# A sliding-window attention with a routed expert layer: keys in a ring, loads and stores on queues of their own, a token table built by matrix products, logits in float32

## The chip, the cores and the metric

The kernel runs on one core of a Trainium2 chip (trn2). The metric is the device time of one execution in microseconds (us), lower is better. The kernel before took 771.98 us in the median of 3 runs (769.98 to 776.52). One more execution was recorded by the profiler; it took 768.93 us.

## What is computed

The reference, cut to what matters:

```python
# q, k, v: (8 batches, 8 heads, 576, 64), float32
scores = q @ k.T / 8
mask_plain = (rel >= 0) & (rel < 32)                       # heads 0 to 3
mask_dil = (rel >= 0) & (rel < 128) & (rel % 4 == 0)       # heads 4 to 7
attn = softmax(where(mask, scores, -1e9)) ; out = attn @ v
x = out.transpose(0, 2, 1, 3).reshape(4608, 512)
logits = x @ w_gate                                        # 8 experts
e = argmax(logits) ; gate = softmax(logits)[e]
y = gate * (relu(x @ w1[e]) @ w2[e])                       # 512 -> 1024 -> 512
```

Each of the 4608 tokens goes to one expert only. Which one depends on the data, so the kernel has to make lists of tokens by expert on the chip.

## The kernel before, in words

There are two stages: 36 tiles of attention with the routing beside them, and then the expert layer.

**Attention.** A tile holds 128 query positions of all 8 heads (two batches side by side, `NPR` = 4 pairs of batches, `NT` = 9 tiles each). `step(n)` (L790) is a pipeline over tiles: in step n PE computes the scores of tile n (`st_scores`, L220, 32 query rows against a window of 64 keys, 16 matmuls), the product with the values of tile n-2 (`st_av`, L267), the transposes of the probabilities of n-1 (`st_trans`), those of the outputs of n-3 (`st_xt`, L317), the logits of n-4 (`st_logits`, L336) and the mask of n+1. DVE computes `nm` (the row maximum), `d` (scores less maximum), `z`, `rz`, `xs` (the normalised output) and `xtl`; ACT computes exp and copies out of PSUM (`pts`, `xth`, `lgs`). The order on PE, DVE and ACT is the program's own up to step 34 (`manual_schedule`, L825); later a scheduler sets it.

SP issues the transfers, in program order: `load(n)` (L164) brings the queries `qt` (256 KB) and, in two transfers, `kvb`: 64 partitions of 640 key columns and 1040 value columns each, where the keys of a tile come with the 32 keys before them. `st_x` (L292) writes the output `xs` to `x_d` in DRAM, in two or three transfers, since the dilated heads (L307 to L315) run through the sequence by residue classes. In `step`, `load(n + 2)` stands behind `st_x(n - 2)`, so on SP the load stands behind the writes. Eight weight tiles of expert 0 (`raw`, 512 KB each) are loaded in between and split into a high and a low part (`wu`).

**Routing.** Logits are computed from a high and a low part of x in a reduced-precision float32 (`xth`, `xtl`, 8 matmuls per tile). After each pair of batches `route` (L388) finds for each token its expert, its gate and its slot (the running place in the list of its expert), in some 15 small DVE operations, spread over the steps (`on_pe`, `off_pe`, `pull_pe`, `pull_off`, L357 to L374). `place` (L425) then scatters a pair (row, gate) of 8 bytes for each token into the DRAM `table`: one indirect DMA on POOL for each tile of 128 tokens, 36 in all. The scatters of three pairs serve the early part of expert 0 (`first`, 3 blocks of 128 tokens), whose `fetch_x` (L568) reads `it` back from `table`, gathers the rows `xg` of `x_d` by it (POOL), and has PE transpose them (`tpx`, L582).

**Experts.** For each expert `layer1` (L608, tile `hps`) and `layer2` (L640, tile `yps`) run over blocks of 128 tokens, with weights and activations split in high and low parts (3 matmuls for one). DVE makes the low parts (`wu` L517, `h` L630). Tokens beyond 512 of an expert go to `Dynamic` blocks (L659), whose table rows and weights are gathered by POOL. `finish` (L550) multiplies by the gate and scatters 128 rows of the output.

Of the kernel before, what the change touches and what calls it, by code (L numbers as in the profile page):

```python
# [9 lines left out]
F32 = mybir.dt.float32  # L10
# [26 lines left out]
KW = P + W  # L37
KC = HP * KW
VC = NB * HP * (DH + 1)
BIG = float(2.0**100)  # L40

SLOTS = 512
CAP = N + SLOTS
# [6 lines left out]
C_ID, C_TRI, C_ONE, C_REV, C_C0, C_BASE, C_THR, C_PU, C_NEW, C_D, C_P = np.cumsum(  # L50
    [0, P, P, P, NE, NE, NE, NTHR, NE, NE * NT, DBLK]
).tolist()
C_ALL = C_P + 1


def _constants():
# [12 lines left out]
    tok = np.zeros((P, NPR, NT, 2), np.int32)  # L69
    tok[:, :, :, 0] = (  # L70
# [5 lines left out]
    slot = np.zeros(((NE + 1) * CAP, 2), np.int32)  # L76
    slot[:, 0] = np.arange((NE + 1) * CAP) % DUMMY

    pos = np.arange(S2) % S
    key = (pos // W * W - W)[:, None] + np.arange(2 * W)[None, :]  # L80
    rel = pos[:, None] - key
    plain = (rel >= 0) & (rel < W) & (key >= 0)
    dil = plain & (key // CLS == (pos // CLS)[:, None])
    mask = np.where(np.stack([plain, dil], axis=1), 0.0, -BIG)
    mask = mask.reshape(NT, P, 2 * 2 * W).transpose(1, 0, 2).reshape(P, -1)
    mask = np.concatenate([np.eye(P), mask], axis=1)
    mask = mask.astype(mybir.dt.np(BF16))
    return dict(cst=c, tok=tok, slot=slot, mask=mask, zero=np.zeros((DUMMY, DM), np.float32))


def _layout(q, k, v, wg, w1, w2):
    perm = np.arange(S).reshape(CLS, DIL).T.reshape(-1)

    def ordered(a):

        a = np.concatenate([a[:, : H // 2], a[:, H // 2 :][:, :, perm]], axis=1)
        return a.reshape(NPR, 2, HP, 2, S, DH).transpose(0, 2, 3, 1, 4, 5).reshape(
            NPR, HP, 2, S2, DH
        )

    def padded(a):
        return np.pad(ordered(a), ((0, 0), (0, 0), (0, 0), (W, 0), (0, 0)))

    qt = ordered(q).reshape(NPR, HP, 2, NT, P, DH).transpose(0, 3, 5, 2, 1, 4)
    kp, vp = padded(k), padded(v)
    kw = np.stack([kp[:, :, :, P * t : P * t + KW] for t in range(NT)], axis=1)
    kw = kw.transpose(0, 1, 3, 5, 2, 4).reshape(NPR * NT, 2, DH, KC)
    vp = np.concatenate([vp, np.ones_like(vp[..., :1])], axis=-1)
# [9 lines left out]
        axis=1,  # L118
    )
    w = np.ascontiguousarray(w).reshape(NE * 8 * P, DF)  # L120
    return dict(
        q=qt.reshape(NPR * NT, P, HP * P), kv=np.concatenate([kw, vw], axis=-1), wg=wgt, w=w
    )

# [896 lines left out]
```

## Time and profile before

| what | value |
|---|---|
| median of 3 runs | 771.98 us |
| profiled execution, its own time | 768.93 us |
| span of that execution, first to last instruction | 767.2 us |
| PE busy | 633.6 us (83% of the span) |
| DVE, ACT, POOL busy | 378.3, 292.7, 186.3 us |
| bytes moved by DMA | 135.77 MB, 177 GB/s in the mean |
| scores of the last tile | about 251 us after the start |
| first matmul of the experts | about 289 us after the start |

Busy time of an engine says little by itself, since the two stages have different limits: the experts keep PE busy without a gap, attention does not. So the profile is read by stage: when the tiles of attention come, what PE waits for between them, what the DMA engines move then, and when the first matmul of the experts starts. "DMA share" is the time that packets took, as a share of 16 engines. "PEclk" is the granted clock as a share of 2.4 GHz; 0.5 is 1.2 GHz.

### The profile page before, as it was taken

What the parts mean: (1) busy time and instruction counts of PE and PEld (TensorE: products, weight loads), DVE (VectorE), ACT (ScalarE), POOL (GpSimd) and SP (SyncE); (2) the same over time, 40 slices, a digit from 0 to 9 for tenths busy, and PEclk for the clock granted to TensorE, in tenths of its full rate; (3) what the DMA queues carried; (4) which work ended last, traced back from release to release, by engine and by line L of the source; (5) the groups of instructions that cost most, each with busy time, mean ns of one, the idle gap of its engine ahead of it and who ended that gap; (6) DMA issues with size and microseconds to landing.
All of it is one profiled execution on the core that took longest, in us unless ns stands there. A gap on an engine that the chain in (4) does not pass through costs nothing. (4 is left out here: it accounts for less than half of the span.)

```text
span 767.2 us, 12980 instructions
## 1 busy us (share of the span) xinstructions
PE 633.6 (83%) x5096; PEld 524.6 (68%) x5096; DVE 378.3 (49%) x708; ACT 292.7 (38%) x564; POOL 186.3 (24%) x184
## 2 busy tenths in 40 slices
PE   4666671765667529999999999999999999999992
PEld 3555661665566429877888888888888888888881
DVE  3555652564355426172663663563654564564410
ACT  1333331332233222262562662653653554554410
POOL 4000031004000414343144044044144134133010
PEclk9999996886687858999999999999999999999997
DMA  8777778778775534254655555565565465565010
GB/s 310 258 248 252 230 229 71 266 257 174 135 256 192 76 102 104 84 166 164 196 202 170 201 193 179 186 211 168 188 214 174 158 228 162 176 229 172 27 42 29
DMA packets 51775, 135.77 MB, mean 177 GB/s; under 512 B 12496, under 2 KB 21840, under 8 KB 51664
## 3 DMA queue, kind: packets, MB, share of 16 engines
q1 hardware_dynamic: 36032, 85.06, 37.7%
q0 software_dynamic: 15680, 49.86, 19.9%
q8 instruction: 41, 0.67, 0.4%
q14 instruction: 22, 0.18, 0.1%
HBM read 115.19 MB, written 20.59 MB: 177 GB/s over the span
## 5 line engine op out<-in xcount | busy, mean ns | idle before, releaser
L517 DVE TENSOR_TENSOR wu<-raw,wu 128x512 fp32r<-128x512 f32 x224 | 144.1, 688 | 81.2 <-ACT wu L516 76.7
L619 PE MATMUL hps<-x,wu 128*128 128x512 f32 (+1 forms) x768 | 179.2, 392 | 2.5 <-DVE h L630 1.9
L649 PE MATMUL yps<-wu,h 128*128 128x512 f32 x744 | 179.4, 396 | 0.0
L619 PEld LDWEIGHTS hps<-x,wu 128*128 128x128 f32 x768 | 144.4, 191 | 31.7 <-DVE h L630 2.3
L649 PEld LDWEIGHTS yps<-wu,h 128*128 128x128 f32 x744 | 139.1, 188 | 31.9
L516 ACT CAST wu<-raw 128x512 fp32r<-128x512 f32 x224 | 126.3, 618 | 75.1 <-DMA raw<-in_w_dram,wi 37.3
L225 PE MATMUL s<-kvb,qt 128*32 128x128 f32 x1152 | 50.0, 327 | 90.6 <-DMA kvb<-in_kv_dram 90.6
L225 PEld LDWEIGHTS s<-kvb,qt 128*32 128x32 f32 x1152 | 38.0, 130 | 100.0 <-issue 88.3
L426 POOL DMA_INDIRECT table<-pay,pos x36 | 36.4, 1012 | 243.5 <-DVE pay L363 158.2
L630 DVE SCALAR_TENSOR_TENSOR h<-hps,h 128x512 fp32r<-128x512 f32 (+1 forms) x64 | 42.8, 672 | 79.6 <-ACT h L629 79.5
L264 ACT COPY pts<-pt 128x512 f32<-128x512 f32 x36 | 21.1, 586 | 158.6 <-PE pt L260 151.5
L692 POOL DMA_INDIRECT raw<-in_w_dram,wi x56 | 56.5, 1009 | 82.4 <-DVE wu L517 70.1
L629 ACT ACTIVATE h<-hps 128x512 fp32r<-128x512 f32 (+1 forms) x64 | 37.0, 582 | 94.1 <-PE hps L619 94.1
L236 DVE TENSOR_REDUCE nm<-s 128x8 f32<-128x512 f32 x36 | 24.8, 689 | 87.1 <-PE s L225 87.1
L554 POOL DMA_INDIRECT out_dram<-y,it x31 | 31.8, 1026 | 133.1 <-DVE y L553 116.9
L274 PE MATMUL o<-kvb,pts 128*32 128x130 f32 x1152 | 50.8, 323 | 0.9 <-DVE xs L295 0.9
L740 PE MATMUL ypd<-wu,hd 128*128 128x512 f32 x192 | 51.4, 405 | 0.0
L542 POOL DMA_INDIRECT xg<-x_d,it x31 | 29.7, 959 | 67.5 <-DMA it<-table 35.9
L709 PE MATMUL hpd<-wu,xd 128*128 128x512 f32 x192 | 46.0, 395 | 0.0
L274 PEld LDWEIGHTS o<-kvb,pts 128*32 128x32 f32 x1152 | 43.1, 132 | 2.3 <-ACT lgs L355 0.9
L553 DVE TENSOR_SCALAR y<-yps,it 128x256 f32<-128x256 f32 x31 | 15.0, 483 | 59.1 <-ACT y L552 59.1
L709 PEld LDWEIGHTS hpd<-wu,xd 128*128 128x128 f32 x192 | 36.0, 188 | 8.7 <-DVE xd L686 0.2
(99 smaller groups left out, 623.4 us busy)
## 6 DMA issues: line engine op xcount, KB each, us to landing
raw<-in_w_dram SPq DMA_DIRECT2D x64, 512.0 KB, 4.6
kvb<-in_kv_dram SPq DMA_DIRECT2D x72, 420.0 KB, 5.3
qt<-in_q_dram SPq DMA_DIRECT2D x36, 256.0 KB, 3.1
x_d<-xs SPq DMA_DIRECT2D x44, 128.0 KB, 3.2
x_d<-xs SPq DMA_DIRECT2D x8, 112.0 KB, 5.3
raw<-in_w_dram,wi POOLq DMA_INDIRECT x56, 5.2
x_d<-xs SPq DMA_DIRECT2D x8, 96.0 KB, 2.3
x_d<-xs SPq DMA_DIRECT2D x8, 80.0 KB, 1.8
```

The source lines that it names most:

```text
L225: nc.tensor.matmul(s[W * j : W * (j + 1), h], lhsT=qt[:, h, W * j : W * (j + 1)], rhs=kt[:, :, o : o + 2 * W], start=False, stop=h == HP - 1,)
L274: nc.tensor.matmul(st["o", n][W * j : W * (j + 1), h // 2, h % 2 * 2 : h % 2 * 2 + 2], lhsT=pts[:, h, W * j : W * (j + 1)], rhs=kt[:, :, a ...
L426: i = nc.gpsimd.indirect_dma_start(out=table, out_offset=bass.IndirectOffsetOnAxis(ap=pos[:, t : t + 1], axis=0), in_=pay[:, b, t, :], in_ ...
L516: nc.scalar.copy(u[:, 0, sl], raw[:, sl])
L517: nc.vector.tensor_tensor(u[:, 1, sl], raw[:, sl], u[:, 0, sl].bitcast(F32), op=ALU.subtract)
L619: nc.tensor.matmul(hps[:, : self.ns], lhsT=u[:, wpart, fs], rhs=self.x[:, xpart, c, : self.ns], start=(k == 0), stop=(k == 11),)
L629: nc.scalar.activation(h[:, 0, :n], hps[:, :n], AF.Relu)
L630: nc.vector.scalar_tensor_tensor(h[:, 1, :n], hps[:, :n], 0.0, h[:, 0, :n].bitcast(F32), op0=ALU.max, op1=ALU.subtract,)
L649: nc.tensor.matmul(yps, lhsT=self.h[f][:, hpart, ts], rhs=u[:, wpart, fs], start=(k == 0), stop=(k == 23),)
L692: nc.gpsimd.indirect_dma_start(out=raw, out_offset=None, in_=w, in_offset=bass.IndirectOffsetOnAxis(ap=self.wi[:, u : u + 1], axis=0),)
L709: nc.tensor.matmul(hps, lhsT=self.x[:, xpart, c], rhs=u[:, wpart, ns], start=(k == 0), stop=(k == 11),)
L740: nc.tensor.matmul(yps, lhsT=self.h[f // 4][:, hpart, f % 4], rhs=u[:, wpart, fs], start=(k == 0), stop=(k == 23),)
```

## The change

- **Keys in a ring.** A tile's 128 keys are loaded once into a ring of 5 places (`kring`); the scores read the 32 keys before them from the neighbour's place (`keys`, an access pattern with a step between the two halves). The dilated heads are laid out so that a tile is 128 consecutive positions for all heads.
- **Queues.** SP carries loads: `load_qk(n + 3)` behind `st_scores(n)`, `load_v(n + 1)` behind `st_av(n - 2)`, queries in 3 buffers, values in 3. `x_d` is written from the ACT queue, in two transfers per tile (`st_xout`).
- **Logits** in plain float32: 4 matmuls per tile into four 32-partition groups, one copy `xt` instead of `xth` and `xtl`, and two copies out (`st_keep`); the sum over the four groups is a product with a 0/1 matrix (`turn`, 9 matmuls for a pair of batches).
- **Table.** Slots are cut in block (slot & -128) and place (slot & 127). For each of 36 tiles DVE makes `s1` (128 x 128, one-hot by place, times the token number) and `b1` (128 x 320, one-hot by block), and PE adds `s1`ᵀ`b1` into `tb` in PSUM; `tbl` sums over the pairs, and `decode` turns it to row numbers `row_i` in SBUF. `table`, its 36 scatters and the reads `it` and `itd` are gone. Gates go to a DRAM column `g_d`, and each block gathers its 128 gates by an indirect DMA (`gates`). Dynamic blocks find their rows in `row_i` by 7 pairs of DVE operations.
- Route's tiles, `d` and `p` have one buffer instead of two.

```diff
-            nc.sync.dma_start(kvb[n % NKV][i::2, i], kv[n, i])
+            nc.sync.dma_start(kring[i::2, n % NK, i], k[n, i])
+
+    def load_v(n):
+        if not 0 <= n < total:
+            return
+        for i in range(2):
+            nc.sync.dma_start(vb[n % NV][i::2, i], v[n, i])
...
+    def st_xout(n):
+        xs, lo = st["xs", n], DUMMY + n * P
+        rows = x_d[lo : lo + P]
+        nc.scalar.dma_start(rows[:, : DM // 2], xs[:, 0].rearrange("p h d -> p (h d)"))
+        nc.scalar.dma_start(
+            rows[:, DM // 2 :].rearrange("(r j) d -> j r d", j=DIL),
+            xs[:, 1].rearrange("p h d -> p (h d)"),
+        )
...
+        def mark(t):
+            s1 = sp.tile([P, P], F32R, name="s1", bufs=3)
+            b1 = sp.tile([P, NBK], F32R, name="b1", bufs=3)
+            v.tensor_scalar(
+                s1,
+                ca[:, C_IO - C_TRI : C_IO + P - C_TRI],
+                plc[:, t : t + 1],
+                pay[:, m, t : t + 1],
+                op0=ALU.is_equal,
+                op1=ALU.mult,
+            )
+            v.tensor_scalar(
+                b1, cc[:, C_BK - C_ATT : C_BK + NBK - C_ATT], blk[:, t : t + 1], None, op0=ALU.is_equal
+            )
...
+                nc.tensor.matmul(box["tb"], lhsT=s1, rhs=b1, start=t == 0, stop=t == NT - 1)
...
+    def gates(it_col, to, rows=N):
+        nc.gpsimd.indirect_dma_start(
+            out=to,
+            out_offset=None,
+            in_=g_d[: DUMMY + rows],
+            in_offset=bass.IndirectOffsetOnAxis(ap=it_col, axis=0),
+        )
...
         go(st_scores, n)
+        load_qk(n + 3)
         go(st_av, n - 2)
+        load_v(n + 1)
...
-        load(n + 2) if n else None
...
+        go(st_xcopy, n - 3)
+        go(st_xout, n - 2)
```

The order on SP in the middle of attention; before, for two tiles (L303 and L311 are the writes of `x_d`):

```order
L303 DMA x_d<-xs 128x256
L311 DMA x_d<-xs 80x256
L311 DMA x_d<-xs 48x256
L168 DMA qt<-in_q_dram 128x512
L170 DMA kvb_105<-in_kv_dram 64x1680 x2
L303 DMA x_d<-xs 128x256
L311 DMA x_d<-xs 96x256
L311 DMA x_d<-xs 32x256
L168 DMA qt<-in_q_dram 128x512
L170 DMA kvb_106<-in_kv_dram 64x1680 x2
```

With the change (L182 queries, L184 keys, L190 values, L652 a weight tile):

```order
L652 DMA raw<-in_w_dram 128x1024
L182 DMA qt<-in_q_dram 128x512
L184 DMA kring<-in_k_dram 64x512 x2
L190 DMA vb_110<-in_v_dram 64x1040 x2
L182 DMA qt<-in_q_dram 128x512
L184 DMA kring<-in_k_dram 64x512 x2
L190 DMA vb_111<-in_v_dram 64x1040 x2
```

No write stands on SP any more, and a tile has five loads there instead of three.

The order on POOL from its first work to the first blocks of expert 0, before:

```order
L176 MEMSET kvb_106 128x3360
L176 MEMSET kvb_107 128x3360
L426 DMA table<-pay,pos 46080x2 x27
L542 DMA xg<-x_d,it 128x512 x3
L426 DMA table<-pay,pos 46080x2 x9
L671 DMA itd<-table,ti_3362 128x2
```

and with the change:

```order
L198 MEMSET vb_111 128x2080
L199 MEMSET wgz 128x128
L586 DMA xg<-x_d,row_i 128x512 x3
L595 DMA gate<-g_d,row_i 128x1 x3
L586 DMA xg<-x_d,row_i 128x512 x2
L595 DMA gated<-g_d,row_i 128x1
```

The 36 scatters are gone, and gathers of gates stand among those of the rows.

The order on DVE where the last pair of batches is routed, beside the first matmuls of the experts. Before (`pos` is the slot, `h` the low part of a result of layer 1, `wu` of a weight):

```order
L466 TENSOR_TENSOR sel<-rk,oh 128x72
L476 TENSOR_TENSOR crun<-crun,cs 128x8
L517 TENSOR_TENSOR wu<-raw,wu 128x512
L469 TENSOR_REDUCE posf<-sel 128x9
L881 TENSOR_TENSOR cnt<-tot,cc 128x8
L363 CAST pos<-posf 128x9
L630 SCALAR_TENSOR_TENSOR h<-hps,h 128x384
```

With the change, the end of the same stretch (the seven pairs of `s1` and `b1` before these stand between `pos` and them):

```order
L440 TENSOR_SCALAR s_3362<-ca,plc,pay 128x128
L448 TENSOR_SCALAR b_3363<-cc,blk 128x320
L440 TENSOR_SCALAR s_3366<-ca,plc,pay 128x128
L448 TENSOR_SCALAR b_3367<-cc,blk 128x320
L504 TENSOR_TENSOR tbl<-tbl,tb 128x320
L515 TENSOR_SCALAR scr<-tbl 128x320
L519 TENSOR_SCALAR none<-tbl,ca 128x320
L516 SCALAR_TENSOR_TENSOR scr<-tbl,scr 128x320
L949 TENSOR_TENSOR cnt<-tot,cc 128x8
L522 TENSOR_TENSOR row_i<-scr,none 128x320
L680 SCALAR_TENSOR_TENSOR h<-hps,h 128x384
```

Before, the first `h` came right behind `pos`; now nine pairs of marks, the sum into `tbl` and the four operations of `decode` stand between the two.

## Rows read from the trace of the kernel before

**Rows 1.** Page, part 2: busy tenths of PE in 40 slices of 19.2 us.

```profile
PE   4666671765667529999999999999999999999992
```

**Rows 2.** Stages: window, its us, busy us of each engine, PEclk, DMA share, GB/s.

```profile
16.00:112.00 96.00, 65.16 (x1275) 56.59 (x1277) 55.88 (x118) 31.69 (x67) 3.73 (x4) 0.91 0.78 253
112.00:137.00 25.00, 8.41 (x146) 6.78 (x141) 6.86 (x13) 4.31 (x9) 5.79 (x6) 0.70 0.83 106
...
181.00:206.00 25.00, 9.70 (x150) 8.72 (x150) 7.20 (x14) 3.36 (x8) 7.66 (x8) 0.62 0.93 160
...
251.20:289.00 37.80, 14.49 (x176) 11.31 (x174) 12.98 (x27) 10.10 (x22) 11.26 (x11) 0.65 0.44 93
...
320.00:767.20 447.20, 431.22 (x1959) 349.41 (x1957) 223.27 (x362) 204.03 (x378) 134.45 (x134) 0.98 0.51 167
```

**Rows 3.** Waits up to 420 us: engine, line, releaser: total us, times, longest.

```profile
PE s L225 <- DMA kvb<-in_kv_dram: 90.6, 27, 16.3
```

**Rows 4.** Timeline of DVE: starts of the row maxima (tiles 3, 18, 19, 26, 28, 35).

```profile
22.09 0.69 DVE L236 TENSOR_REDUCE nm<-s 128x8 f32<-128x512 f32 x1 [1.60 <-PE s L225]
...
116.73 0.69 DVE L236 TENSOR_REDUCE nm<-s 128x8 f32<-128x512 f32 x1 [0.62 <-PE s L225]
...
137.18 0.69 DVE L236 TENSOR_REDUCE nm<-s 128x8 f32<-128x512 f32 x1 [12.32 <-PE s L225]
...
179.87 0.68 DVE L236 TENSOR_REDUCE nm<-s 128x8 f32<-128x512 f32 x1
...
204.79 0.69 DVE L236 TENSOR_REDUCE nm<-s 128x8 f32<-128x512 f32 x1 [8.28 <-PE s L225]
...
252.60 0.68 DVE L236 TENSOR_REDUCE nm<-s 128x8 f32<-128x512 f32 x1
```

**Rows 5.** Waits of SP up to 300 us, same columns.

```profile
SPq L303 <- DVE xs L295: 106.2, 34, 6.8
```

**Rows 6.** Timeline of SP: start, us, what; one tile's writes.

```profile
48.83 0.33 SPq L303 DMA_DIRECT2D x_d<-xs  x1
49.21 0.95 SPq L311 DMA_DIRECT2D x_d<-xs  x2
```

**Rows 7.** DMA issues: line, engine, xcount, KB each, median us to landing.

```profile
kvb<-in_kv_dram SPq DMA_DIRECT2D x72, 420.0 KB, 5.3
...
x_d<-xs SPq DMA_DIRECT2D x44, 128.0 KB, 3.2
...
table<-pay,pos POOLq DMA_INDIRECT x36, 14.0
```

**Rows 8.** Stages of 2 us at the start, columns as in rows 2.

```profile
14.00:16.00 2.00, 2.00 (x34) 1.53 (x27) 1.04 (x4) 0.63 (x1) 0.00 (x0) 1.00 1.14 466
```

**Rows 9.** Timeline of PE: two masks, one step apart.

```profile
44.79 0.39 PE L211 MATMUL s<-mk 128*128 128x512 bf16 x1
...
48.42 0.39 PE L211 MATMUL s<-mk 128*128 128x512 bf16 x1
```

**Rows 10.** Timeline, all engines, from attention's end to the first expert matmul.

```profile
273.00 0.39 SPq L571 DMA_DIRECT2D it<-table  x1
...
275.83 0.97 POOL L542 DMA_INDIRECT xg<-x_d,it  x1 [13.84 <-DMA it<-table]
...
280.65 1.12 PE L582 MATMUL tpx<-ident,xg 128*128 128x128 f32 x4 [14.50 <-DMA xg<-x_d,it]
...
289.02 1.33 PE L619 MATMUL hps<-x,wu 128*128 128x384 f32 x3 [0.68 <-ACT x L585]
```

**Rows 11.** Groups up to 300 us: line, engine, shapes, xcount | busy us, mean ns.

```profile
L331 DVE TENSOR_TENSOR xtl<-tp,xth 128x512 fp32r<-128x512 f32 x36 | 24.9, 691 | 26.5 <-ACT xth L326 25.7 <-issue 0.6
...
L444 DVE TENSOR_TENSOR sh<-lg,mx 128x72 f32<-128x72 f32 x4 | 0.9, 224 | 0.0
...
L883 DVE TENSOR_TENSOR over<-cnt,cc 128x320 f32<-128x320 f32 x1 | 0.5, 480 | 0.0
```

**Rows 12.** Groups from 289 to 320 us, same columns.

```profile
L619 PE MATMUL hps<-x,wu 128*128 128x384 f32 x96 | 19.3, 359 | 0.7 <-ACT x L585 0.7
```

More of the change, by code (lines that the diff above doesn't have):

```diff
@@ L218, in st_mask, with keys @@
         st["s", n] = s
+    def keys(n, h, j):
+        here, last = n % NK, (n - 1) % NK
+        cols = slice(h * P + W * j, h * P + W * (j + 1))
+        if h < HP // 2 and j:
+            return kring[:, here, :, h * P + W * (j - 1) : h * P + W * (j + 1)]
+        own = kring[:, here, :, cols]
+        before = kring[:, last, :, cols] if h >= HP // 2 else kring[:, last, :, (h + 1) * P - W : (h + 1) * P]
+        (part, rows), (head, two), (one, _) = own.ap
+        step = own.offset - before.offset
+        return bass.AP(own.tensor, before.offset, [[part, rows], [head, two], [step, 2], [one, W]])
     def st_scores(n):
-        s, qt, kt = st["s", n], qts.pop(n), kvb[n % NKV]
+        s, qt = st["s", n], qts.pop(n)
         for h in range(HP):
             for j in range(NB):
-                o = h * KW + W * j
                 nc.tensor.matmul(
@@ L419, in rank @@
             )
-            nc.tensor.matmul(
-                rk, lhsT=cc[:P, C_TRI : C_TRI + P], rhs=oh, start=False, stop=False
-            )
-            nc.tensor.matmul(rk, lhsT=one, rhs=cs, start=False, stop=True)
-        def place(t):
-            i = nc.gpsimd.indirect_dma_start(
-                out=table,
-                out_offset=bass.IndirectOffsetOnAxis(ap=pos[:, t : t + 1], axis=0),
-                in_=pay[:, b, t, :],
-                in_offset=None,
-            )
-            tc.declare_no_dep(i.ins, group="slots", reason="slots are handed out once")
-            need(i, [table_init])
-            tc.add_to_no_dep_group("slots", i.ins)
-            scatters.append(i)
@@ L569, in fetch_x @@
             e = self.e
-            self.it = sp2.tile([P, 4, 2], I32, name="it")
-            i = nc.sync.dma_start(
-                self.it[:, : self.nblk],
-                table[e * CAP : e * CAP + self.ns].rearrange("(i p) t -> p i t", p=P),
-            )
-            need(i, scatters)
-            self.xg = [gather(self.it[:, i, 0:1], self.rows) for i in range(self.nblk)]
+            self.it = [row_i[:, e * BPE + i : e * BPE + i + 1] for i in range(self.nblk)]
+            self.xg = [gather(it, self.rows) for it in self.it]
+            self.gate = sp2.tile([P, 4], F32, name="gate")
+            for i, it in enumerate(self.it):
+                gates(it, self.gate[:, i : i + 1], self.rows)
             self.x = pools["x", e % 2].tile([P, 2, 4, SLOTS], F32R, tag="x", name="x")
```

411 lines of the change are left out of this document (219 added, 192 removed).

## The prediction, made blind

> **What bounds the kernel now.** I read the page first, for where PE is not busy [rows 1]: in slices 1 to 15 it is 40 to 70% busy, with two holes at slices 7 and 10 and one at slice 14, and from slice 16 on it is full. So the kernel is attention, some 250 us, a hole of nearly 40 us, and then the experts, which PE bounds: from 320 us to the end it is busy 431.22 us of 447.20, and most of what is left over is the drain of the last stores [rows 2].
>
> Next the stages. While the tiles of attention run undisturbed (16 to 112 us), PE is busy 65 us of 96 and DVE 56; neither is full. The DMA share is 0.78, at 253 GB/s [rows 2]. The waits say who is late: PE stood 90.6 us before the scores for `kvb`, in 27 waits [rows 3]. That SP had not issued the loads earlier is seen in its own queue: before the write of `x_d` it waited 106.2 us for `xs`, 34 times [rows 5], and the load of tile n+2 stands behind that write. So a load starts late in step n, needs 5.3 us to land [rows 7], and must be there at the start of step n+2.
>
> The row maxima give the pace: from tile 3 at 22.09 to tile 18 at 116.73 us are 15 steps of 6.31 us [rows 4]. A step in which PE waits for nothing is 48.42 - 44.79 = 3.63 us [rows 9].
>
> The holes at slices 7 and 10 are the scatters. Tile 18 to 19 took 20.45 us and tiles 26 to 28 24.92 us [rows 4], against 6.31 and 12.62: together 26.4 us lost. In these stretches the DMA share is 0.83 and 0.93 while only 106 and 160 GB/s move, PE is busy 8 to 10 us of 25, and PEclk falls to 0.70 and 0.62, after PE had stood idle [rows 2]; a scatter needs 14.0 us to land [rows 7]. So writes of 8 bytes take the DMA engines from the loads of the keys.
>
> The third hole is the way into the experts. The scores of tile 35 are there before 252.60 us [rows 4], but `it` is read from the table at 273.00 only, when the third pair's scatters have landed; the gather goes out at 275.83, its first transposes run at 280.65 and the first expert matmul at 289.02 [rows 10].
>
> **The change, part by part.** The sum is made against the profiled execution's own 768.93 us, which lies 3.05 us under the median of the runs (771.98); I add these at the end.
>
> *Scatters out.* 26.4 us of attention go, and with them the wait for `table` in the third hole. The page does not separate what they cost outside the three intervals; I take nothing for that.
>
> *Loads and writes apart.* Three loads of lead and no write in front: then PE no longer waits for a late issue, and what is late next is the DMA engines. In the undisturbed stretch they were busy 0.78 x 96 = 74.9 us [rows 2] for 96 / 6.31 = 15.2 tiles, 4.92 us per tile, a weight tile now and then included. The ring leaves out 128 rows of 128 columns of 4 bytes, 66 KB of 253 x 96 / 15.2 = 1.60 MB; at the rate of a stretch with loads alone (466 GB/s at share 1.14, so 409 GB/s at 1.00 [rows 8]) that is 0.16 us. So 4.76 us per tile at a share of 1.00. I take 4.9 us, a share of 0.97, since the queues always hold loads for the next tiles but starts are not even. Bounds: 4.2 us if the share of 1.14 in rows 8 can be kept up (4.76 / 1.14), and 6.3 us if nothing is gained. The value is near the first reading because the wait of rows 5 has no counterpart on SP afterwards.
>
> The Trainium skill, page "DMA: Bandwidth & Descriptors", section "Issuing engines are not separate DMA queues", says that transfers started by several engines share the same 16 DMA engines, and that a second issuing engine saves only the issue time. The trace agrees that the 16 are shared, since table writes slowed loads from another queue [rows 2]; but it shows a wait of 3.1 us per write in front of the loads (106.2 / 34, rows 5), which is no issue time. By the page only 0.33 + 0.95 us per tile [rows 6] would go, a pace of 5.03 us, and the total below would be 4 us longer.
>
> *Do the engines stay below 4.9 us?* DVE has 55.88 / 15.2 = 3.68 us per tile now [rows 2]. `xtl` goes (0.69 us, rows 11). Marks come: two operations per tile of tokens, 36 times. The trace has no operation of their kind; by the nearest, 0.224 us for 72 columns and 0.480 for 320 [rows 11], I take 0.28 for `s1` (128 columns) and 0.48 for `b1`. With one addition into `tbl` and small ones that is 8.3 us for 9 tiles, 0.92 per tile: DVE comes to 3.9 us. They stand in about four of nine steps, which then have about 5.1 us; three loads of lead carry over that. PE loses four logits matmuls and gains the products (320 columns; 19.3 / 96 = 0.20 us each by the 384-column matmuls of rows 12) and nine for the logits of a pair, together some 4 us per nine tiles, and comes to 4.1 us from 3.63. ACT has 31.69 / 15.2 = 2.1 us and takes over two issues per tile, 0.33 to 0.95 us [rows 6]; a write there waits for `xs`, and behind it stand the copies of the logits, for which only the next steps wait. All of this hides under the DMA pace, and costs its excess if the pace fell under it.
>
> So: tile 3 comes at about 20 us (22.09 now [rows 4]; keys alone have to land first, I estimate 2 us), and tile 35 at 20 + 32 x 4.9 = 177 us, instead of 252.60.
>
> *The way into the experts.* `row_i` of the first three blocks is decoded on DVE just before the row maximum of tile 35. From the issue of the gather to the transposes were 4.8 us and from there to the first expert matmul 8.4 us [rows 10], together 13.2: 177 + 13 = 190 us, instead of 289.02. The reading of `it` is gone.
>
> *The first expert.* On DVE the first low part `h` stood right behind the slots of the last pair; now 18 marks, one addition and four decodes of 128 x 320 stand in between, 6.8 + 5 x 0.48 = 9.2 us. PE has three buffers of layer 1, 36 matmuls or 7.2 us [rows 12], and is used to a shorter chain. I take 9 us as exposed. Bounds: nothing, if PE's own work covers it, and 16 us, if the 14 lookups of the dynamic blocks (14 x 0.48 = 6.7 us) come to stand in front of the later `h` as well.
>
> *Experts.* 39 gathers of gates are added on POOL, and 7 gathers of table rows go. POOL was busy 134.45 us of 447 there, 1.0 us for each of 134 [rows 2]; 32 more make 166. PE does not wait for them: a gate is wanted only when a block's results are done. I take 0.
>
> Sum: 190 + (768.93 - 289.02) + 9 = 679 us for a profiled execution, and 679 + 3 = 682 us for the median.
>
> **Rivals.**
>
> *A. DMA is not the limit; the engines are.* For it: 466 GB/s was reached [rows 8]. Against it: that was loads alone, without writes. The pace would be 4.2 us: tile 35 at 154, the experts at 167, the total 659 us.
>
> *B. The loads do not come earlier in effect.* The change would then not do what it says: five transfers of 256 KB or less take the place of three, and ACT, busy itself, issues the writes. For it: the DMA share was 0.78 already. Against it: rows 3 and 5 show waits for an issue. The pace stays 6.3 us; scatters and the third hole still go. Tile 35 comes at 222, the experts at 235, the total is 727 us.
>
> *C. The gates' gathers hold POOL in the expert stage, and the kernel gets slower.* Dynamic weights and rows are issued on the same queue behind them. POOL has 447 - 134 = 313 us to spare there [rows 2], 8.0 us for each of 39 gathers. If a gather of 4-byte entries held the queue for as long as a scatter took to land, 14.0 us [rows 7], 39 would need 546 us, 233 more than there is, and the total is 915 us. It decides from 10.5 us per gather on: (313 + 98) / 39, where 98 us eat up the gain. Against it: POOL went on 1.0 us after each issue.
>
> **How the numbers follow.** The forecast has a chance of 0.66, with a range of its own of 662 to 706 (a pace of 4.4 to 5.5 us, and 4 to 14 us at the first expert). A has 0.16, B 0.15, C 0.03. A lower end of 646 is A without the loss at the first expert; an upper end of 728 is B, and leaves out half of it and C. About 1% is what a measurement of this kernel can tell from no change. All cases but C are faster by far more; with a little for an unseen cost in attention that eats the gain: faster 0.95, the same 0.02, slower 0.03.
>
> **What would show it right or wrong.** Right: row maxima 4.9 us apart from tile 3 to tile 35 with no gap of 10 us or more; a DMA share of 0.95 or more in the middle of attention; SP no longer waiting for `xs`; the first `hps` at about 190 us; a wait of PE of some 9 us for `h` behind DVE within 20 us of that, and from there to the end about 460 us of full PE. Wrong: a pace near 6.3 with PE waiting for `kring` or `vb` (B); PE waiting for DVE's marks instead of loads in attention (the engines bound, at a longer pace than A's); weights that land late in the expert stage behind the gates (C).

## The result, and the profile after

The changed kernel took 737.43 us (median of 4 runs, 734.85 to 739.58), against 772.65 us for the kernel before on the same chip: a ratio of 0.954 [0.949, 0.959]. It is faster, by two fifths of what was foretold (35 us instead of 90): 682 us was said, with a range of 646 to 728, and the result lies above the range. The profiled execution has a span of 733.0 us.

The page of the changed kernel, part 2 (40 slices of 18.3 us):

```profile
PE   4678878878877898989999999999999999999992
...
PEclk9879899899979899999999999999999999999997
DMA  7678867876865042546744754763663674564010
```

The two holes of [rows 1] at slices 7 and 10 are gone, as foretold. But DMA stands at 6 to 8 tenths through attention, where 0.97 was said. Attention from 16 to 112 us in one stretch, columns as in [rows 2]:

```profile
16.00:112.00 96.00, 73.37 (x1277) 55.34 (x1271) 48.19 (x120) 36.75 (x79) 0.00 (x0) 0.86 0.75 243
```

Before, this stretch read 65.16 us of PE, a DMA share of 0.78 and 253 GB/s [rows 2]: the loads come no faster. The granted clock of PE is 0.86 in this stretch, so it spends part of it at the lower of its two levels (1.2 and 2.4 GHz). The starts of the row maxima (DVE's timeline; tiles 3, 18, 19 and 35) answer to [rows 4]:

```profile
21.91 0.69 DVE L260 TENSOR_REDUCE nm<-s 128x8 f32<-128x512 f32 x1 [2.30 <-PE s L249]
...
116.62 0.68 DVE L260 TENSOR_REDUCE nm<-s 128x8 f32<-128x512 f32 x1
...
118.98 0.68 DVE L260 TENSOR_REDUCE nm<-s 128x8 f32<-128x512 f32 x1
...
223.32 0.69 DVE L260 TENSOR_REDUCE nm<-s 128x8 f32<-128x512 f32 x1 [3.17 <-remote]
```

Tile 3 to tile 18 is 15 steps of 6.31 us, to the hundredth the pace before; all 32 steps to tile 35 are (223.32 - 21.91) / 32 = 6.29 us, since no step of 20 us is among them any more. Who holds the loads is in SP's own queue (waits up to 300 us; total, times, longest), which answers to [rows 5]:

```profile
SPq L182 <- DMA x_d<-xs: 32.7, 8, 6.7
...
SPq L190 <- DMA x_d<-xs: 16.4, 7, 5.1
SPq L184 <- DMA x_d<-xs: 14.8, 5, 4.3
SPq L652 <- DMA x_d<-xs: 10.8, 5, 4.2
```

SP no longer waits for `xs`. It waits 74.7 us, 25 times, for the *landing* of writes that ACT issued. No data joins a load of queries to a write of `x_d`. PE in turn waits for what is issued late (waits up to 420 us; in `e1_writes_pool`, below, the same two are 5.5 and 2.3 us up to tile 35):

```profile
PE s L249 <- DMA kring<-in_k_dram: 20.3, 15, 2.8
...
PE o L298 <- DMA vb<-in_v_dram: 12.6, 14, 2.7
```

One such wait of SP in the timelines of ACT, SP and PE:

```profile
63.77 0.32 ACTq L329 DMA_DIRECT2D x_d<-xs  x1
64.23 0.53 ACTq L330 DMA_DIRECT2D x_d<-xs  x1
...
64.59 1.17 SPq L190 DMA_DIRECT2D vb<-in_v_dram  x2
70.06 0.33 SPq L182 DMA_DIRECT2D qt<-in_q_dram  x1
...
75.00 1.08 PE L249 MATMUL s<-kring,qt 128*32 128x128 f32 x32 [1.72 <-DMA kring<-in_k_dram]
```

and the DMA engines beside it (windows of 2 us):

```profile
66.00:68.00 2.00, 2.00 (x40) 1.64 (x40) 1.82 (x3) 0.43 (x2) 0.00 (x0) 1.00 0.85 269
68.00:70.00 2.00, 1.77 (x42) 1.07 (x41) 1.30 (x5) 1.36 (x3) 0.00 (x0) 1.00 0.26 99
```

SP has issued everything up to 65.8 us and then nothing for 4.3 us, until the write of 64.23 has landed; the DMA engines run dry (0.26), and then PE waits for the keys. The compiled program says why. A completion semaphore is a counter that a transfer raises when it has landed. These are rows of SP's order and of ACT's, each engine for itself, with the semaphores that each row waits for:

```
SP   L190 DMA vb_109<-in_v_dram 64x1040 [waits DMAHW3_49,PE_49]
SP   L190 DMA vb_109<-in_v_dram 64x1040 [waits DMAHW6_49,DMAHW4_49]
SP   L182 DMA qt<-in_q_dram 128x512 [waits DMAHW7_49,PE_49]
ACT  L329 DMA x_d<-xs 128x256 [waits DMAHW6_49,DVE_49]
ACT  L330 DMA x_d<-xs 4x32x256 [waits DMAHW7_49]
```

SP's and ACT's transfers take eight completion semaphores (DMAHW0 to 7) in one common turn, and each waits until the transfer that had its semaphore eight places earlier has landed. Here the queries have DMAHW7 eight places behind ACT's second write, the one of 64.23. A tile has seven transfers, so the turn shifts from tile to tile: in the compiled order 23 loads of queries, keys and values and 11 weight tiles take a semaphore that last belonged to a write from ACT. SP runs ahead of ACT, so that write is issued late, seen from SP.

The way into the experts and the first expert (timelines of PE, DVE):

```profile
240.19 0.79 PE L669 MATMUL hps<-x,wu 128*128 128x384 f32 x3 [0.68 <-ACT x L635]
...
249.79 0.39 DVE L448 TENSOR_SCALAR b<-cc,blk 128x320 fp32r<-128x320 f32 x1
...
257.25 0.49 DVE L522 TENSOR_TENSOR row_i<-scr,none 128x320 int32<-128x320 f32 x1
257.66 0.55 DVE L680 SCALAR_TENSOR_TENSOR h<-hps,h 128x384 fp32r<-128x384 f32 x1
```

The first expert matmul comes 16.9 us after tile 35's maximum (240.19 - 223.32) instead of 36.4 [rows 4, 10], and from it to the end are 492.8 us instead of 478.2: 14.6 more. The marks and the decode of the last pair stand on DVE from 249.79 on, in front of the first `h`, as foretold. But PE does not stand for `h` all that time: from 240.2 to 262 it is busy 20.30 of 21.80 us, with the sum of the logits (3.35 us), the ranks and the products `tb` between those of layer 1, and with a granted clock of 0.50 (1.2 GHz) from 242 to 248. The first 36 products of layer 1 are done after 13.8 us, against 9 us before the change.

What the prediction named for its upper bound came as well. The lookups of the dynamic blocks (`tf`) stand on DVE in front of a later `h`, and PE waits for it:

```profile
274.61 0.55 DVE L918 SCALAR_TENSOR_TENSOR tbl<-cc,sl,row_i 128x320 f32<-128x320 f32 x1
...
280.22 0.55 DVE L680 SCALAR_TENSOR_TENSOR h<-hps,h 128x384 fp32r<-128x384 f32 x1
...
280.83 3.77 PE L699 MATMUL yps<-wu,h 128*128 128x512 f32 x15 [3.52 <-DVE h L680]
```

### The profile page after: what moved, and what is told of

It reads as the page before. It is cut to its first block, busy times and chain, and to the rows that moved or that the text cites. A ratio compares the mean times of both kernels' runs of the same rounds, so it can differ in the third digit from the quotient of the medians.

```text
span 733.0 us, 13283 instructions
## 1 busy us (share of the span) xinstructions
PE 651.9 (89%) x5172; PEld 519.2 (71%) x5172; DVE 375.6 (51%) x777; ACT 307.2 (42%) x604; POOL 184.5 (25%) x181
## 5 line engine op out<-in xcount | busy, mean ns | idle before, releaser
L669 PE MATMUL hps<-x,wu 128*128 128x512 f32 (+1 forms) x768 | 183.1, 395 | 3.7 <-DVE h L680 2.7
L586 POOL DMA_INDIRECT xg<-x_d,row_i x32 | 32.8, 1026 | 281.0 <-DVE row_i L522 242.7
L732 POOL DMA_INDIRECT raw<-in_w_dram,wi x56 | 58.1, 1037 | 67.5 <-DVE wu L561 55.0
L606 POOL DMA_INDIRECT out_dram<-y,row_i x32 | 34.1, 1065 | 143.0 <-DVE y L605 114.8
L298 PE MATMUL o<-vb,pts 128*32 128x130 f32 x1152 | 50.9, 324 | 17.9 <-DMA vb<-in_v_dram 12.6
L249 PE MATMUL s<-kring,qt 128*32 128x128 f32 x1152 | 46.6, 308 | 20.3 <-DMA kring<-in_k_dram 20.3
L298 PEld LDWEIGHTS o<-vb,pts 128*32 128x32 f32 x1152 | 40.7, 130 | 23.2 <-issue 12.0
L249 PEld LDWEIGHTS s<-kring,qt 128*32 128x32 f32 x1152 | 34.9, 122 | 29.8 <-issue 14.7
L604 ACT ACTIVATE y<-yps,gate 128x256 f32<-128x256 f32 x31 | 14.6, 473 | 62.4 <-PE yps L699 59.0
L605 DVE TENSOR_SCALAR y<-yps,gate 128x256 f32<-128x256 f32 x31 | 14.9, 481 | 49.3 <-ACT y L604 40.8
```

What stands on the lines that cost most here:

```text
L249: nc.tensor.matmul(s[W * j : W * (j + 1), h], lhsT=qt[:, h, W * j : W * (j + 1)], rhs=keys(n, h, j), start=False, stop=h == HP - 1,)
L298: nc.tensor.matmul(st["o", n][W * j : W * (j + 1), h // 2, h % 2 * 2 : h % 2 * 2 + 2], lhsT=pts[:, h, W * j : W * (j + 1)], rhs=vt[:, :, a ...
L606: nc.gpsimd.indirect_dma_start(out=out, out_offset=bass.IndirectOffsetOnAxis(ap=it_col, axis=0), in_=y, in_offset=None,)
L669: nc.tensor.matmul(hps[:, : self.ns], lhsT=u[:, wpart, fs], rhs=self.x[:, xpart, c, : self.ns], start=(k == 0), stop=(k == 11),)
L732: nc.gpsimd.indirect_dma_start(out=raw, out_offset=None, in_=w, in_offset=bass.IndirectOffsetOnAxis(ap=self.wi[:, u : u + 1], axis=0),)
```

## The experiments

All ratios are against the kernel before on the same chip. To tell attention from what follows, each run is split at the last row maximum: "tile 35" is its start, "pace" is (tile 35 - tile 3) / 32, "rest" is the span less tile 35. In e2, e3, e6 and e8 the table is not filled, so every block gathers and writes the same 128 dummy rows; these four are prices of a part, not kernels to use, and what the dummy rows themselves change in the rest is not known.

| run | median us | ratio [95%] | tile 35 | pace | rest |
|---|---|---|---|---|---|
| before | 772.65 | 1 | 252.6 | 7.20 | 514.6 |
| changed | 737.43 | 0.954 [0.949, 0.959] | 223.3 | 6.29 | 509.7 |
| e1_writes_pool | 683.57 | 0.890 [0.884, 0.896] | 184.5 | 5.12 | 497.3 |
| e2_no_marks | 720.26 | 0.936 [0.927, 0.944] | 221.2 | 6.24 | 499.6 |
| e3_before_no_scatters | 719.30 | 0.936 [0.930, 0.942] | 228.1 | 6.39 | 489.7 |
| e4_writes_sp | 692.77 | 0.903 [0.896, 0.911] | 191.0 | 5.32 | 498.0 |
| e5_eighth | 732.40 | 0.953 [0.947, 0.960] | 227.7 | 6.43 | 500.3 |
| e6_pool_no_marks | 666.00 | 0.865 [0.860, 0.871] | 163.5 | 4.45 | 500.4 |
| e7_pool_lead2 | 695.63 | 0.904 [0.897, 0.911] | 198.5 | 5.38 | 496.8 |
| e8_before_pool | 666.27 | 0.867 [0.861, 0.873] | 175.0 | 4.77 | 487.1 |
| e9_loads_pool | 706.55 | 0.921 [0.914, 0.928] | 202.6 | 5.57 | 500.2 |
| e10_pool_late_loads | 682.80 | 0.889 [0.883, 0.895] | 185.9 | 5.12 | 494.1 |
| e11_pool_b1 | 694.94 | 0.903 [0.899, 0.908] | 192.9 | 5.36 | 500.6 |
| e12_before_writes_pool | 725.94 | 0.938 [0.930, 0.947] | 205.0 | 5.67 | 520.0 |
| e13_loads_pool_later_write | 722.49 | 0.932 [0.924, 0.941] | 204.9 | 5.68 | 519.8 |
| e14_later_write | 736.08 | 0.950 [0.942, 0.959] | 220.0 | 6.22 | 515.2 |
| e15_pool_spread | 682.00 | 0.883 [0.875, 0.891] | 179.6 | 4.96 | 493.6 |
| e16_loads_pool_writes_sp | 710.93 | 0.927 [0.921, 0.933] | 192.3 | 5.27 | 515.1 |
| e17_pool_spread3 | 683.23 | 0.889 [0.882, 0.896] | 171.3 | 4.70 | 510.6 |

### Who issues the writes

`e1_writes_pool` and `e4_writes_sp` change one word in `st_xout` of the changed kernel:

```diff
-        nc.scalar.dma_start(rows[:, : DM // 2], ...)
+        nc.gpsimd.dma_start(rows[:, : DM // 2], ...)    # e1; nc.sync in e4
```

> The changed kernel with the writes of x_d issued by POOL, which is idle in attention, instead of ACT; nothing else. Theory 1 (shared completion semaphores: a load on SP may only be issued when the transfer that had its semaphore 8 transfers earlier has landed, and that is a write of x_d, so the writes still hold the loads back): SP's waits for x_d, 75 us in the changed kernel, go; the pace falls from 6.3 to about 5.2 us per tile, and the total by 25 to 45 us, to 695 to 712 us. Theory 2 (the DMA engines are full): the pace stays, total within 1% of 737 us. Theory 3 (PE, with the products and logits of the routing in its order and half its clock in places, sets the pace): the pace stays, total within 1%.

> The changed kernel with the writes of x_d issued by SP again, at their place in the program, behind which the next step's loads then stand. Theory 1: the loads waited for the writes already, so little changes: total within 1.5% of 737 us. The prediction's reasoning (a queue of its own takes the wait for xs away from the loads): the pace is lost again, and the total rises by 20 us or more, to 757 us or above. Theory 2: within 1%.

With the writes on POOL the kernel takes 683.57 us, 54 less, and the pace is 5.12; theory 1 has the direction, and its 695 us were still too many. The same stretch, the whole of tiles 3 to 35, and SP's longest wait (up to 200 us):

```profile
16.00:112.00 96.00, 85.87 (x1709) 66.13 (x1702) 62.06 (x149) 48.39 (x107) 26.03 (x40) 0.98 0.94 322
...
20.80:184.53 163.73, 143.48 (x2701) 109.75 (x2705) 107.50 (x288) 80.16 (x180) 43.31 (x67) 0.95 0.87 293
```

```profile
SPq L182 <- PE s L249: 20.7, 9, 5.2
```

The engines move 322 GB/s instead of 243, and SP waits for PE to free a buffer, not for a write: that is nearly the attention that was foretold. PE's granted clock is 0.98 there instead of 0.86, so part of the gain is PE's own. On SP, in front of the next step's loads, the writes cost 9 us more than on POOL, but still 45 less than on ACT; all three expectations for e4 fall. So in the changed kernel a write in the way of the loads is not what hurts. On SP a write is issued in its turn: 16 loads of queries still have a semaphore that last belonged to a write, but SP's waits for `x_d` are small, and so is what is left of the wait for `xs` (up to 210 us):

```profile
SPq L329 <- DVE xs L318: 11.6, 6, 4.4
...
SPq L330 <- DMA x_d<-xs: 3.0, 5, 1.1
...
SPq L182 <- DMA x_d<-xs: 2.3, 3, 1.2
```

### Is it the common turn of semaphores?

`e5_eighth` adds an eighth transfer to a tile of the changed kernel, at the end of `step`:

```diff
+        if n % 4 != 1 and n < total:
+            nc.sync.dma_start(tiny[:, n : n + 1], cst[:1, n : n + 1])
```

> The changed kernel, with one tiny load (4 bytes, on SP) added at the end of each step of attention that loads no weight tile. The compiled program gives the hardware transfers of SP and ACT together eight completion semaphores in turn, and each transfer waits until the one that had its semaphore eight transfers before has landed. A tile of the changed kernel has seven transfers, so its query load waits for a write of the tile before; with eight, a load waits for the same load of the tile before, and a write for a write (in about one tile of three the second half of the values still waits for a write). Nothing else differs. Theory 1 (what holds the loads back is this turn of semaphores): SP's waits for the landing of x_d, 75 us in the changed kernel, fall under 35, the pace goes from 6.29 to between 5.0 and 5.7 us, tile 35 comes at 182 to 205 us, the total is 688 to 715 us. Theory 2 (writes from ACT's queue are slow or late in themselves, or collide with the loads in the DMA engines): the pace stays at 6.2 or more, the total is 737 us within 1%, since four bytes change nothing in the engines.

Nothing came of it: 732.40 us, a pace of 6.43. But the edit did not do what it was made for. In the compiled order 21 loads of queries, keys and values (23 in the changed kernel) still follow a write from ACT on their semaphore, 17 of them loads of values, and SP still waits 70 us for `x_d`:

```profile
SPq L191 <- DMA x_d<-xs: 48.1, 11, 7.5
...
SPq L183 <- DMA x_d<-xs: 9.9, 3, 4.7
SPq L878 <- DMA x_d<-xs: 7.4, 2, 3.8
```

Since the wait stayed, the run says nothing for or against it. `e9_loads_pool` separates the two in another way: ACT keeps its writes, and POOL, whose transfers have semaphores of their own in the compiled program (DMASW0 to 7), issues the loads inside the loop. (It also takes them out from behind the weight tiles on SP, which still wait for writes; that part is not separated.)

```diff
-        load_qk(n + 3)
+        load_qk(n + 3, nc.gpsimd)
...
-        load_v(n + 1)
+        load_v(n + 1, nc.gpsimd)
```

> The changed kernel with its writes of x_d on ACT as they are, but with the loads of queries, keys and values inside the loop of attention issued by POOL instead of SP. POOL's transfers have completion semaphores of their own, so no such load waits for a write (the weight tiles on SP still can). Theory 1 (sharing the eight semaphores with ACT's writes is what holds the loads back): the pace goes from 6.29 to between 4.9 and 5.6 us, the total is 680 to 710 us. Theory 2 (a write issued by ACT is late or slow in itself, and takes the loads' time whoever issues them): the pace stays at 6.0 or more, the total is 725 us or more.

706.55 us, a pace of 5.57, and tile 35 at 202.6 instead of 223.3, although the start is 2.4 us later (tile 3 at 24.27). What POOL waits for (up to 210 us) is a free buffer:

```profile
POOL qt L182 <- PE s L249: 69.1, 28, 6.9
```

So 21 of the 39 us between the changed kernel and e1 at tile 35 go with the shared semaphores; ACT's writes by themselves do not hold these loads back. What is still missing in e9, 18 us, three more runs looked for:

> As e9 (loads in the loop on POOL, writes on ACT; 706.6 us), but in step n ACT issues the write of tile n-3 instead of that of n-2, in front of the copy xt: xs was made a step earlier, so ACT need not stand for it. Theory 1 (the 23 us between e9 and e1 are ACT standing at the write for xs, with the copies that PE waits for behind it): pace 5.0 to 5.3 us, total 680 to 694 us. Theory 2 (they are what loads issued by POOL cost, or the write's wait for its own semaphore): pace 5.45 or more, total 700 to 712 us.

> As the changed kernel (loads on SP, writes on ACT, 737 us), but in step n ACT issues the write of tile n-3 instead of that of n-2. About as many loads share their semaphore with a write as in the changed kernel (29 against 27 of those looked at). Theory 1 (the two parts add: sharing, 31 us, stays, and ACT standing for xs, 23 us, goes): 705 to 725 us. Theory 2 (the loads' waits for the landing of writes set the pace alone, and ACT's standing is hidden behind them): 730 to 745 us.

> As e9 (loads in the loop on POOL), with the writes of x_d issued by SP instead of ACT. Theory 1 (the 23 us between e9, 706.6, and e1, 683.6, are what loads issued by POOL cost, whoever writes): 700 to 712 us. Theory 2 (they are what writes issued by ACT cost in ACT's own queue, sharing set aside): 680 to 693 us.

```diff
+        go(st_xout, n - 3)          # e13 (on e9) and e14 (on the changed kernel)
         go(st_xt, n - 3)
         go(st_xcopy, n - 3)
-        go(st_xout, n - 2)
...
-        nc.scalar.dma_start(rows[:, : DM // 2], ...)
+        nc.sync.dma_start(rows[:, : DM // 2], ...)      # e16 (on e9)
```

e13 does not bring tile 35 forward (204.9 against 202.6), and its total, 722.49 us, is above both expectations, since the rest grows; e14 moves tile 35 by 3 us (220.0 against 223.3) and the total not at all. By its total e16 fits "what POOL's loads cost", but the split says otherwise: tile 35 comes at 192.3, 10 us sooner than in e9, and the total is lost in the rest (515.1 against 500.2).

Where these 10 us stand can be read from what PE waits for. In e9 it waits for results of ACT (waits up to 210 us):

```profile
PE o L298 <- ACT p L276: 6.8, 5, 2.0
PE lt L394 <- ACT lgs L363: 6.3, 3, 2.4
```

In e16, up to tile 35, the same two lines are 0.7 and 0.9 us. So an ACT that issues the writes delivers its probabilities and its copies of the logits later, and PE stands 11.5 us longer for them. e13, which was to cure that, does bring the two down, to 1.5 us each; but PE then waits 12.4 us (0.5 in e9) in front of the same product with the values, for something that the profile does not name. So the run does not settle what a write issued a step later is worth.

Of the 39 us, then, 21 come back with separate semaphores and some 10 when ACT no longer issues the writes. The last 8 (192.3 in e16 against 184.5 in e1) are not assigned: e16 and e1 have loads and writes the other way round on SP and POOL, and e16 is within 1.4 us of e4 (191.0), which has both on SP.

### What the lead and the ring are worth

`e10_pool_late_loads` is e1 with the loads back at the end of the step:

```diff
-        load_qk(n + 3)
-        load_v(n + 1)
...
+        load_qk(n + 2) if n else None
+        load_v(n + 1) if n else None
```

> The changed kernel with the writes of x_d on POOL (683.6 us), and with the loads at the end of the step, as before: queries and keys of tile n+2 and the values of n+1 at the end of step n, instead of those of n+3 at its start and of n+1 behind the product with the values of n-2. (The run e7_pool_lead2, which loaded the values of n+2 there, overwrote a buffer still to be read, so that the product waited for a load of its own step: its 695.6 us are an upper bound for this one.) Theory 1 (the longer lead matters): pace 5.5 us or more, total 695 us or more. Theory 2 (once nothing stands in front of the loads, the lead is worth nothing, as the old kernel with its writes on POOL suggests, whose pace is 4.77 us): pace within 0.15 of 5.12, total within 1% of 683.6 us.

682.80 us, the same pace of 5.12: the longer lead is worth nothing once no load waits for a write. (In e7, which loads the values of n+2 there, the product takes values of a later tile.)

> The changed kernel with the writes of x_d on POOL (683.6 us), and with the loads put back to the lead of before: queries, keys and values of tile n+2 at the end of step n (instead of n+3 for queries and keys at its start, and n+1 for the values behind the product with the values of n-2). Theory 1 (the lead matters, as the prediction argued with a load that starts late and needs 5.3 us): the pace rises to 5.6 us or more, the total to 700 us or more. Theory 2 (it is enough that no load stands behind a write or waits for one): the pace stays within 0.15 of 5.12, the total within 1% of 683.6 us.

e7 takes 12.8 us more than e10, and PE waits 12.6 us there for values: that is the wait for a load of its own step. `e8_before_pool` asks the same of the kernel before, e12 does it with the scatters left in:

```diff
-        nc.sync.dma_start(
+        nc.gpsimd.dma_start(        # the writes in st_x; e8 and e12
             xb[t * P : (t + 1) * P, : DM // 2], xs[:, 0].rearrange("p h d -> p (h d)")
...
-        for t in range(NT):         # e8 and e3
-            off_pe(place, t)
```

> The kernel before without the scatters into the table (719.3 us, the rows of the experts are then dummy rows, as there), and with its writes of x_d issued by POOL instead of SP; loads, keys and logits as before. Theory 1 (the waits of SP for xs in front of the loads are what held the pace at 6.3 us, [rows 5] against the pace): the pace falls to 5.0 to 5.5 us, tile 35 comes at 184 to 202 us, the total is 675 to 695 us. Theory 2 (the ring of keys and the longer lead are needed): pace 5.8 us or more, total 705 us or more.

719.30 became 666.27 us, pace 4.77: moving the writes off SP gives 53 us to the old kernel, without a ring, without a longer lead, with its logits in two parts.

There is a second way to the same end, though. e3 and e4 both have their writes on SP; e3, the old kernel without scatters, has a pace of 6.39, and e4, the changed kernel, 5.32, although only e4 makes marks. SP's wait for `xs` is 94.3 us in e3 (up to 230 us) and 11.6 in e4. So with the writes left on SP the longer lead, the ring and the new order take most of that wait away. Which of them does it, no run separates.

And with everything else left as it was:

> The kernel before, whole, with nothing changed but that its writes of x_d are issued by POOL instead of SP: the scatters into the table stay, on the same engine. Theory 1 (the two gains, from the scatters and from the writes, are separate: without scatters the writes on POOL took 719.3 down to 666.3 us, 53 us): 770 less 53, within 710 to 730 us. Theory 2 (POOL's scatters hold up the writes behind them and with them xs and the products, so that part of the gain is lost): 735 to 770 us.

725.94 us: this one word, in the two calls that write `x_d`, is worth no less in the kernel before than the whole change (0.938 [0.930, 0.947] against 0.954 [0.949, 0.959]).

### What the scatters cost, and what the table

> The kernel before without its 36 scatters into the table, which keeps its initial dummy rows; reads and gathers stay. The prediction's price of the scatters: 26.4 us in the pace of attention, and the wait for the table in front of the first gather, some 10 us; total 772 - 36 = 736 us, the same as the changed kernel, so that everything else of the change came to nothing in sum. If the scatters cost less than that, the total stays above 750 us.

e3 leaves out the call of `place` (diff above). 719.30 us: 24.5 us at tile 35 (252.6 to 228.1) and 25 us in the rest. Of the 25, 19.6 are the way into the experts, where the wait for the table was (36.4 to 16.8 us), and 5.3 come behind the first `hps`, for a reason that no run shows. The 36 us of the expectation were too few. And e3 is 18 us faster than the changed kernel, so all else in the change, with the table that takes the scatters' place, cost time in sum.

> The changed kernel without the 36 pairs of one-hot matrices, their products and the sums into the table, which is set to zero instead: all rows gathered are then the 128 dummy rows, as many as before. Theory 3: the routing steps are what makes the pace, so attention becomes 25 us or more shorter, total at or under 705 us. Theories 1 and 2: attention gains at most 8 us, and the first expert some 8 us since its low parts no longer stand behind the marks; total 721 to 732 us.

```diff
-                off_pe(mark, t)
-            on_pe(enter, ts, late=True)
...
+            off_pe(v.memset, tbl, 0.0)      # e2; e6 on e1
```

The pace stays (6.24), the rest falls by 10.1 us.

> The changed kernel with the writes of x_d on POOL (683.6 us), and without the one-hot matrices, their products and the additions into tbl (tbl is zero, so every block gathers and writes the dummy rows: the routing of tokens is left out). Theory 1 (the table costs only at the first expert, as the prediction says, 9 us with bounds 0 and 16; without it the changed kernel gained 17 us): the pace stays at 5.12 within 0.15, the total is 667 to 675 us. Theory 2 (with the loads no longer held back, the marks on DVE and PE set the pace in part): pace 4.9 or less, tile 35 at 177 us or sooner, total 662 us or less.

With the loads set free the same edit brings tile 35 from 184.5 to 163.5 us: the marks then cost 21 us of attention, of which the way into the experts gives back a part (from tile 35 to the first `hps` 23.8 us against 15.9). How busy the DMA engines can then be is seen from e6's tiles 3 to 35, a share of 0.98:

```profile
21.01:163.50 142.49, 130.14 (x2666) 100.42 (x2667) 92.24 (x238) 79.48 (x180) 41.78 (x66) 0.99 0.98 335
```

The marks' extra time stands in single steps of 8 us at the ends of pairs. One of them, in e9 (PE, then DVE):

```profile
135.26 0.96 PE L458 MATMUL tb<-b,s 128*128 128x320 f32 x2 [0.66 <-DVE b L448]
138.24 0.41 PE L458 MATMUL tb<-b,s 128*128 128x320 f32 x1 [2.02 <-DVE b L448]
138.59 1.72 PE L249 MATMUL s<-kring,qt 128*32 128x128 f32 x32
```

```profile
136.94 0.69 DVE L575 TENSOR_TENSOR wu<-raw,wu 128x512 fp32r<-128x512 f32 x1 [1.18 <-ACT wu L572]
137.55 0.34 DVE L440 TENSOR_SCALAR s<-ca,plc,pay 128x128 fp32r<-128x128 f32 x1
137.81 0.38 DVE L448 TENSOR_SCALAR b<-cc,blk 128x320 fp32r<-128x320 f32 x1
```

PE has the products `tb` in front of the scores of the next tile; they wait for `b1`, and in DVE's order a low part of a weight tile, which waits for ACT, stands in front of it. In e1 the same step takes 8.05 us (119.66 to 127.71); there the low part waits only 0.22 us for ACT, and the products stand behind the six pairs of marks themselves.

> The changed kernel with the writes of x_d on POOL (683.6 us), and with one of the two marks of each tile of tokens, b1 (128 x 320), made by POOL instead of DVE, a candidate for a better version. Theory 1 (the marks are exposed because they lengthen DVE's chain in the steps at the end of a pair and in front of the first h; without any marks the kernel takes 666.0 us): about half of the 17.6 us comes back, total 670 to 679 us. Theory 2 (POOL takes several times DVE's 0.38 us for b1, and the products wait for it, or the writes of x_d stand behind it): 684 us or more.

> The changed kernel with the writes of x_d on POOL (683.6 us), and with the marks and products of the first two pairs of batches spread out: two tiles of tokens per step, the products behind the mask, instead of six per step. The last two pairs are as they were. Theory 1 (a step with six marks is bound by DVE, some 8 us, and with two it fits under the pace of the loads): the steps of 8 us at tiles 16 to 18 and 25 to 27 fall under 6.5 us, tile 35 comes 5 to 14 us sooner than 184.5, total 670 to 679 us. Theory 2 (marks cost their sum wherever they stand): within 1% of 683.6 us.

> As e15 (writes on POOL, marks of the first two pairs spread, 682.0 us in the median of runs from 675.0 to 685.1), with the products of the third pair's marks also one group per step, behind the mask. Theory 1 (its steps of 8 to 9 us before tile 35 go, and the fetch for the first expert is not held up): 672 to 680 us. Theory 2 (the early fetch waits for the third pair's table, so the way into the experts grows by what the steps gain): within 1% of 682 us.

```diff
-            v.tensor_scalar(
+            nc.gpsimd.tensor_scalar(           # e11, b1
...
-            on_pe(enter, ts, late=True)
+            on_pe(enter, ts, late=m >= 2)      # e15, two tiles for m < 2; e17: late=m == 3
```

POOL is no help (694.94 us): it takes 1108 ns in the mean for `b1`, DVE 382 in e1, and PE waits for it; `s1` on DVE beside it takes 428 ns instead of 339. Spread out, the steps of 8 us at tiles 16 to 18 and 25 to 27 go (at most 5.4 us there in e15), and tile 35 comes at 179.6 and 171.3. The total is 682.00 and 683.23 us, not told apart from e1's 683.57: in e17 the gather for the first expert goes out 7 us behind tile 35's maximum (at 178.29), in e1 1 us ahead of it (183.42), and the first `hps` stands at 200.36, in e1 at 200.39. The best versions are e1, e10, e15 and e17, 0.883 to 0.890 of the kernel before.

## Why the prediction was wrong, point by point

- **Scatters out: right.** 26.4 us in attention were said; e3 shows 24.5. The wait for the table in the third hole went too (36.4 to 16.8 us in e3).
- **The pace: wrong, and this is the step that failed.** 4.9 us was taken, "near the first reading because the wait of rows 5 has no counterpart on SP afterwards". It had one: SP's 106.2 us before `xs` became 74.7 us before the landing of writes, through the common turn of semaphores, and the pace of 6.29 is the upper bound, "if nothing is gained". The mechanism behind the 4.9 holds where the wait is really gone: 5.12 us in e1, with a DMA share of 0.94 in the stretch from 16 to 112 us, and 4.45 us at a share of 0.98 in e6. That e1's 683.57 us lie 1.6 us from the forecast is in part luck: tile 35 comes 7.5 us later than said and the way in is 2.9 us longer, while the experts take 5.8 us less. The term 4.76 us per tile at a share of 1.00 was too large: over tiles 3 to 35 e1 needs 0.87 x 5.12 = 4.45, e6 0.98 x 4.45 = 4.36.
- **The lead: not separated from the queue.** "Three loads of lead and no write in front" were named together. With the writes on POOL the lead is worth nothing (e10), and e8 (4.77) beside e6 (4.45) leaves at most 0.3 us per tile for lead, ring and logits together. With the writes on SP it may be worth something (e4 against e3); that is not shown by itself.
- **The marks in attention: hidden, it was said; 21 us at tile 35 when the loads are free** (e1, e6). That "three loads of lead carry over that" was wrong, since the products of the marks stand in PE's own order in front of the next scores, and no load that is there early shortens that. With ACT's writes in the way the marks cost 2 us at tile 35 (e2).
- **The rule of the Trainium skill.** The Trainium skill, page "DMA: Bandwidth & Descriptors", section "Issuing engines are not separate DMA queues", says that a second issuing engine saves only the issue time; by it the pace was to be 5.03. In the changed kernel POOL as a second engine agrees (5.12 against 5.32 with all on SP: 0.20 us, less than the issue time). In the old kernel it does not: 6.39 became 4.77 (e3, e8), 1.62 us, where the issues take 0.33 + 0.95 [rows 6]. Nor does ACT as a second engine: 6.29 against 5.32, a loss of about 1 us per tile. The measurement decides: it matters which engine, what stands behind the write there, and which semaphores it shares.
- **The way into the experts:** 13 us said, 16.9 measured (15.9 in e1). A term under-sized by 4.
- **The first expert:** 9 us said, with bounds 0 and 16; 14.6 measured from the first `hps` to the end. Without the marks this stretch is 13.3 us shorter (479.5 in e2), but the way in is 3.3 us longer there, so the marks cost 10.1 us in the rest. The place was right; the foretold sign, a wait of PE of some 9 us for `h`, did not come in that form, since PE was busy 20.30 of 21.80 us there with other products and at a lower clock. The total is near the upper bound because part of what was named for it, the lookups in front of a later `h`, came in too (3.5 us).
- **Experts otherwise: 0 said.** Without marks the changed kernel needs 479.5 and 476.6 us from the first `hps` to the end (e2, e6), the old one 472.9 and 469.8 (e3, e8): some 7 us for gates, lookups and the rest, which no run separates.
- **Rival B** came nearest (727, at a pace of 6.3 and tile 35 at 222), with the words "loads do not come earlier in effect". Of its reason half was there: ACT, busy itself, does issue the writes late. How a late write can hold a load was not in it, and that the transfers are more and smaller was not what hurt (e1 has the same ones). A and C did not occur.

Sum of the miss, in spans: tile 35 at 223 instead of 177 (46 us), the way in 4, from the first `hps` to the end 6 (492.8 instead of 478.2 + 9): 677 became 733.

What stays open: the last 8 us between e16 and e1 at tile 35, and in part why the rest is 487 to 501 us in some of these kernels and 510 to 520 in others. In two of the long ones (before, e12) it is the wait for the table, 36 and 40 us from tile 35 to the first `hps`. In the other five (changed, e13, e14, e16, e17) PE waits 3.2 to 3.7 us for the `h` behind the lookups, and in no other run over 1 us there; but that is only a part of the 10 to 20 us.

## What to carry to other kernels

Before moving transfers to another engine, read in the compiled order which completion semaphore each transfer waits for: where two queues take them in one common turn, the engine that runs ahead waits for the landing of what the other issues late (74.7 us here). Change one word (who issues the writes) before building a ring; here that word alone, in the kernel before, was worth no less than the whole change. And split every result at the end of a stage, since a gain in one can be lost in the next.

## What was not expected of the hardware and the program

- The same writes, issued by POOL, SP or ACT, give 683.6, 692.8 and 737.4 us.
- SP and ACT share eight completion semaphores in turn; POOL has others. A load waited up to 6.7 us for a write that has nothing to do with it.
- `b1` (128 x 320, a comparison) takes 1108 ns on POOL (e11) and 382 ns on DVE (e1).
